# Gated mix of two attentions on one core: the rows of the q/k projection in another order, so that four of its five tiles are stored whole

## The chip, the core and the metric

The kernel runs on one core of one Trainium2 chip. The metric is device time in microseconds (us) for one execution. A core has five engines that each work through their own queue of instructions in order: TensorE (PE, matrix products; PEld is its loading of weights), VectorE (DVE), ScalarE (ACT), GpSimd (POOL), and SyncE (SP), which in this kernel issues every DMA. They wait for each other through semaphores.

## The reference

One input `x` (2048 tokens of 640 channels) goes through two attention blocks with 32 heads of 20 channels, and a sigmoid gate mixes the two results.

```python
def _A_ref(x, wq, wk, wv, wo, beta):          # 4 segments of 512 tokens
    q, k, v = x @ wq, x @ wk, x @ wv          # split into heads and segments
    phi = lambda t: where(t > 0, t + 1.0, exp(t))
    for s in range(4):
        p = softmax(qs @ ks.T * scale + mask) # inside the segment, key after query masked
        a_dot = p @ vs
        a_mem = (phi(qs) @ M) / (phi(qs) @ z + 1e-6)
        o = g * a_mem + (1 - g) * a_dot       # g = sigmoid(beta), one a head
        M, z = M + phi(ks).T @ vs, z + sum(phi(ks))
    return concat(o) @ wo
def _B_ref(x, wqkv, wo):                      # causal, window of 256 keys
    return softmax(windowed(q @ k.T * scale)) @ v @ wo
g = sigmoid((x * gate_w).sum(-1))
return g * a + (1 - g) * b                    # a, b: results of the two blocks
```

(Reshapes into heads and segments are left out.)

## The kernel before

**Tiles and units.** Work is cut by segment (`s`, 512 tokens) and by group of 16 heads (`g`: 0 and 1 are the two halves of block A, 2 and 3 of block B). One such pair is a T; there are 16, in the order g = 0, 2, 1, 3 in each segment. A T has four units `u` of four heads each, so 64 units. A T needs five q/k tiles `m` of 128 rows by 512 tokens (640 rows: 320 of q, 320 of k) and four v tiles.

**Exact products.** Most products run in a 32-bit format with fewer mantissa bits. Each operand is therefore split in a high part and a low rest (`split_h`, L516 or L518, and `split_l`, L532), and three products are added. `gemm2` (L578) and `v_mm` (L730) use only 64 of the array's 128 rows; two of them, one on each row half, run at the same time. Which instruction stands next to which in PE's queue thus decides whether both halves are filled. The probability times value product (`av_mm`, L919) and the small memory products (`mem_read` L946, `mem_add` L966) use strips of 128 x 32, and no half product runs beside them.

**From projection to scores.** A finished q/k tile goes from the accumulation bank to SBUF as a pair of parts, `ml[:, 0]` high (`m_high`, ACT, L599) and `ml[:, 1]` low (`m_low`, DVE, L603). SP stores it to DRAM in an image where every head has 20 rows high, 20 rows low and 20 rows high again; q holds high, low, high and k high, high, low, so that one product over 60 rows gives all three terms. The image has 160-row pieces, and tiles have 128 rows, so `runs_of` cuts a tile into one or two runs, eight in a T, and `qk_store` issues two DMAs for each run: L635 stores high and low to two places, L633 stores the high part again. That makes 16 DMAs for a T. `stack_read` (L804, L807, L809) reads a unit's rows back into `qks`. `max_mm` (L833) computes scores, `max_red` (L843, DVE) their row maxima, which go through DRAM (L859, L863) into two more rows of `qks`; `st_mm` (L887) then computes scores less the maximum, `st_exp` (L894, ACT) the exponential.

**Memory of block A.** `phi_neg`, `phi_exp`, `phi_sum` (L640, L644, L648) make phi of a q/k tile, `phi_store` (L657) writes it by the same runs to `dphi`, `mem_query` (L933) reads phi of q back in eight DMAs for two units, `mem_load` (L927) phi of k.

**Loading.** `load` (L524) brings weight tiles (`wst`, two buffers) and pieces of x (`xst`, four buffers); at the start the five pieces of the first segment go through the four `xst` buffers.

**What sets the order.** No loop order is written by hand. Each step is put into a list with a due time, an engine, a duration, and the buffers that it reads and writes; `Plan.order` then simulates the engines and takes, for the engine that can start first, the waiting step with the lowest rank. A rank is the due time, shifted by tables by kind of step and time (`SHIFT`, and `NUDGE` in slots of 12.5 us). The order in which steps are taken is the order of every queue. SP's queue has at most eight DMAs in flight: each waits for the one eight before it.

## Time and profile before

| | us |
|---|---|
| median of 3 runs | 988.43 |
| lowest, highest | 983.97, 991.27 |
| profiled execution, its own time | 980.1 |
| span of its instructions | 978.4 |
| PE, DVE, ACT, POOL busy | 967.9, 761.4, 651.7, 637.2 |
| PEld busy | 812.6 |
| granted clock | 1.000 |
| DMA | 248.56 MB, mean 254 GB/s |

The profile is of one execution. A row of a group gives the line, engine, operation, what is written and read, the count, then the busy time with the mean of one in ns, and then the engine's idle time just before, with what ended it. Ends of products on PE are modelled, and products on the two row halves overlap, so a PE that is busy all the time can still have one half empty.

### The profile page before, as it was taken

Reading aid. Unit: us, or ns where it says so; the run is one execution under the profiler, and the core shown is the slowest. Engines: PE = TensorE matmul, PEld = TensorE weight load, DVE = VectorE, ACT = ScalarE, POOL = GpSimd, SP = SyncE. Lnnn points to the kernel's source line nnn. Section 1 sums busy time; section 2 is a strip of 40 time slices with the busy share of each in tenths; the row PEclk is TensorE's granted clock in tenths of the full one; section 3 lists DMA queues with packets and bytes.
Section 4 is the critical chain, followed back from the end, with each engine's and each line's share of the span. In section 5 each row is a group of like instructions: output and inputs, shape, how many; then the busy total and the mean of one; then the engine's idle time right before and its main releaser. Section 6 shows DMA issues by size and latency. Waiting matters only on the chain.

```text
span 978.4 us, 30482 instructions
## 1 busy us (share of the span) xinstructions
PE 967.9 (99%) x11295; PEld 812.6 (83%) x11295; DVE 761.4 (78%) x2626; ACT 651.7 (67%) x1432; POOL 637.2 (65%) x864
## 2 busy tenths in 40 slices
...
GB/s 276 306 306 267 290 277 275 252 293 265 279 260 283 277 220 308 205 314 298 260 264 242 254 280 207 311 224 333 285 230 234 222 296 270 137 268 215 180 99 103
DMA packets 158036, 248.56 MB, mean 254 GB/s; under 512 B 52032, under 2 KB 68288, under 8 KB 157888
## 3 DMA queue, kind: packets, MB, share of 16 engines
...
## 4 chain that ended last, share of the span: by engine, by line
PE 92%; DVE 3%; DMA 3%; ACT 0%; issue 0%; POOL 0%; SPq 0%; DVEq 0%
PE bank L578 43%; PE bank L919 15%; PE bank L730 14%; PE bank L833 9%; PE bank L887 8%; DVE bank L843 2%; PE bank L570 2%; DMA wst<-wqk 1%; PE bank L946 1%; PE bank L966 1%; DMA wvs<-wv 1%; DMA xst<-xt 1%; DVE mx L843 0%; DVE ot L990 0%; SPq L524 0%
## 5 line engine op out<-in xcount | busy, mean ns | idle before, releaser
L894 ACT ACTIVATE P<-bank 128x512 f32<-128x512 f32 (+2 forms) x768 | 381.3, 556 | 148.2 <-PE bank L887 98.2
L578 PE MATMUL bank<-xhl,w 64*128 64x512 f32 x2400 | 453.5, 398 | 3.6 <-ACT xhl L516 2.8
L578 PEld LDWEIGHTS bank<-xhl,w 64*128 64x128 f32 x2400 | 325.4, 186 | 14.8 <-ACT xhl L516 3.7
L833 PE MATMUL bank<-qks 60*128 60x384 f32 (+3 forms) x1024 | 309.1, 334 | 1.3 <-DVE ot L990 0.8
L843 DVE CUSTOM_DVE_ANT_0 bank<-bank,mask_b 128x384 f32<-128x384 f32 (+2 forms) x512 | 259.7, 553 | 28.3 <-PE bank L833 21.1
L730 PE MATMUL bank<-wv,xhl 64*128 64x320 f32 (+1 forms) x1920 | 280.6, 313 | 0.2 <-POOL wv L532 0.2
L843 DVE CUSTOM_DVE_ANT_0 bank<-bank,mask_a 128x128 f32<-128x128 f32 (+3 forms) x512 | 239.9, 509 | 39.4 <-PE bank L833 29.2
L887 PE MATMUL bank<-qks 62*128 62x384 f32 (+3 forms) x1216 | 261.1, 301 | 0.4 <-DVE ot L990 0.2
L730 PEld LDWEIGHTS bank<-wv,xhl 64*128 64x128 f32 x1920 | 238.8, 186 | 3.2 <-issue 1.2
L578 PE MATMUL bank<-ohl,w 64*128 64x512 f32 x1050 | 226.3, 399 | 0.1
L532 POOL TENSOR_TENSOR w<-wst,w 128x640 fp32r<-128x640 f32 x112 | 174.9, 1565 | 77.9 <-ACT w L516 77.0
L900 POOL TENSOR_SCALAR_AFFINE_SELECT P<-P 128x512 f32<-128x512 f32 x256 | 161.5, 640 | 76.7 <-ACT P L894 71.6
L887 PEld LDWEIGHTS bank<-qks 62*128 62x128 f32 x1216 | 195.8, 185 | 15.3 <-issue 3.3
L833 PEld LDWEIGHTS bank<-qks 60*128 60x128 f32 x1024 | 177.5, 184 | 20.8 <-issue 6.2
L919 PE MATMUL bank<-P,vau 128*32 128x384 f32 (+3 forms) x2432 | 159.9, 407 | 0.2
L578 PEld LDWEIGHTS bank<-ohl,w 64*128 64x128 f32 x1050 | 152.9, 185 | 8.6 <-issue 3.3
L843 DVE DVE_READ_ACCUMULATOR2_ANT mx<- 128x1 f32 x1024 | 142.5, 139 | 0.0
L919 PEld LDWEIGHTS bank<-P,vau 128*32 128x32 f32 x2432 | 69.3, 110 | 78.6 <-issue 63.5
L516 ACT ACTIVATE w<-wst 128x640 fp32r<-128x640 f32 x121 | 89.4, 741 | 40.1 <-PE bank L578 15.7
L990 DVE STREAM_TRANSPOSE ot<-bank 128x512 f32<-128x512 f32 x64 | 45.8, 715 | 64.0 <-PE bank L919 61.6
L903 POOL TENSOR_SCALAR_AFFINE_SELECT P<-P 128x512 f32<-128x512 f32 x112 | 70.8, 641 | 4.5 <-ACT P L894 4.1
L532 POOL TENSOR_TENSOR wv<-wvs,wv 128x322 fp32r<-128x322 f32 x80 | 65.2, 834 | 11.8 <-ACT wv L516 11.5
...
## 6 DMA issues: line engine op xcount, KB each, us to landing
...
```

Of the source, the lines that this page charges most:

```text
L516: nc.scalar.activation(dst, src, AF.Copy)
L532: EN[e].tensor_tensor(out=t[:, 1], in0=B.pop(src), in1=f(t[:, 0]), op=ALU.subtract)
L578: z = nc.tensor.matmul(B[key], B[wkey][64 * r:64 * r + 64, a, 128 * c:128 * c + 128], B[xkey, c][64 * r:64 * r + 64, b], start=start, stop ...
L730: z = nc.tensor.matmul(B["v", T, b][:, :n], B[("x", s), c][64 * r:64 * r + 64, a, 128 * b:128 * b + 128], B["wv", T, c][64 * r:64 * r + 64 ...
L833: nc.tensor.matmul(psum(("mx", u, p, b, r))[:, :n], fr(q), keys(u, 3 * DH, r, p, c0, n), start=True, stop=True)
L843: nc.vector.tensor_tensor_reduce(out=x, in0=x, in1=mk, scale=1.0, scalar=BIG, op0=ALU.add, op1=ALU.max, accum_out=B["M", u][:, j:j + 1])
L887: nc.tensor.matmul(B[k][:, c:c + 128 * n], keys(u, K, r, p, WIN + 128 * kb, 128), fr(q[64 * r:64 * r + K, L * p + 128 * q0:L * p + 128 * ( ...
L894: nc.scalar.activation(B["P", u, b][:, 2 * r + p, c0:c1], B["st", u, b, p, r][:, c0:c1], AF.Exp, scale=SCALE)
L900: nc.gpsimd.affine_select(out=v, in_=v, pattern=[[0, 4], [1, 128]], compare_op=ALU.is_ge, fill=0.0, base=0, channel_multiplier=-1)
L903: nc.gpsimd.affine_select(out=v, in_=v, pattern=[[0, 4], [-1, 128]], compare_op=ALU.is_gt, fill=0.0, base=0, channel_multiplier=1)
L919: nc.tensor.matmul(o[32 * j:32 * j + 32, 128 * q0:128 * (q0 + n)], v[:, VA * h:VA * h + 32], t[:, j, c:c + 128 * n], start=(b == 0 and i = ...
L990: nc.vector.transpose(t, B["o", u])
```

## The change

The columns of the q/k weights are laid out anew, which gives the rows of the projection another order. For a group of 16 heads, tiles 0 and 1 now hold the first 16 channels of q, eight heads each (16 x 8 = 128 rows, one half of the image); tiles 3 and 4 the same for k. Tile 2 holds the last four channels of q (64 rows) and of k (64 rows).

- `qk_store`: a whole tile takes two DMAs. One writes the high part to its two places at once, by reading the same source twice; the other writes the low part. Tile 2 takes six DMAs of 64 rows. A T has 14 instead of 16, all T's together 224 instead of 256. The store of the high part no longer waits for `m_low`: a step may now ask for the `first` writer of a buffer alone.
- `phi_store`: one DMA a tile, two for tile 2 where both are wanted; 36 instead of 48. `mem_query`: six DMAs for two units instead of eight, 72 instead of 96. `dphi` and `mem_add` use the new row order.
- The five pieces of x for the first segment go into the five `ys` buffers, which are free then.
- The planner: `join` (a marker between the two halves of an accumulation) is planned shorter, `NUDGE` is looked up by finer groups of steps (`GROUPS`), and its numbers are all new. So the order of every queue is new.

The products, the conversions and the bytes of each are the same in number; SP's list falls from 1042 DMAs to 974.

```diff
--- before
+++ after
@@ -77,31 +77,44 @@
+GROUPS = dict(
...
-    a={22: 0.6},
...
+    c={7: 1.3, 31: -0.8, 32: -1.4, 39: 1.5, 66: 3.8},
...
@@ -238,6 +254,11 @@
                     deps[i] |= s["free"] if name[0] in ("qk", "qf", "pk") else {s["base"]}
                 s["puts"].append(i)
             for name in get:
+                if name[0] == "first":
+                    s = slot(name[1])
+                    deps[i].add(s["base"])
+                    s["gets"].append(i)
+                    continue
                 s = slot(name)
                 assert s["puts"] or s["base"] is not None, (fn, a, name)
                 deps[i] |= set(s["puts"])
...
@@ -520,6 +541,7 @@
 
     def load(tag, pool, bufs, width, key, src):
         B[key] = (xpool.tile([128, L], F32, name=tag, tag=tag, bufs=bufs)[:, :width] if tag == "xst" else
+                  work.tile([128, L], F32, name=tag, tag=tag, bufs=bufs) if tag == "ys" else
                   pool.tile([128, width], F32, name=tag, tag=tag, bufs=bufs))
         nc.sync.dma_start(B[key], src)
 
...
@@ -602,16 +624,9 @@
         t = B["ml", k]
         nc.vector.tensor_tensor(out=t[:, 1], in0=B[k], in1=f(t[:, 0]), op=ALU.subtract)
 
-    def runs_of(m, kinds=(0, 1)):
-
-        out, r = [], 0
-        while r < 128:
-            z, at = divmod(128 * m + r, QB)
-            n = min(QB - at, 128 - r)
-            if z // 2 in kinds:
-                out.append((*divmod(z, 2), at, r, n))
-            r += n
-        return out
+    PARTS = ((0, 0), (0, 1), None, (1, 0), (1, 1))
+    PIECES = [[(0, 128, 0), (0, 128, 1)], [(0, 128, 0), (0, 128, 1)], [(64 * w, 64, i) for i in range(3) for w in range(2)],
+              [(0, 128, 0), (0, 128, 1)], [(0, 128, 0), (0, 128, 1)]]
 
     def image(T, w):
 
...
@@ -622,17 +637,24 @@
         d = dkb[g - 2] if w else dqb[T // 2 % 2]
         return (d, S, d.offset + L * s) if w else (d, L, d.offset)
 
-    def qk_store(T, m, n, twice):
-
-        w, half, at, r, c = runs_of(m)[n]
+    def qk_store(T, m, n):
+
+        r, c, i = PIECES[m][n]
+        w, half = PARTS[m] or (r // 64, 0)
         d, row, off = image(T, w)
-        ml = f(B["ml", ("m", T, m)][r:r + c])
-        z = (2 - 2 * w) if twice else w
-        off += (512 * half + 8 * DH * z + at) * row
-        if twice:
-            nc.sync.dma_start(bass.AP(tensor=d.tensor, offset=off, ap=[[row, c], [1, L]]), ml[:, 0])
+        step = 8 * DH * row
+        if c == 128:
+            x = f(B["ml", ("m", T, m)])[:, i]
+            off += 512 * half * row + (2 - w) * step * i
+            if i:
+                nc.sync.dma_start(bass.AP(tensor=d.tensor, offset=off, ap=[[row, 128], [1, L]]), x)
+            else:
+                nc.sync.dma_start(bass.AP(tensor=d.tensor, offset=off, ap=[[row, 128], [(1 + w) * step, 2], [1, L]]),
+                                  bass.AP(tensor=x.tensor, offset=x.offset, ap=[list(x.ap[0]), [0, 2], [1, L]]))
         else:
-            nc.sync.dma_start(bass.AP(tensor=d.tensor, offset=off, ap=[[row, c], [8 * DH * row, 2], [1, L]]), ml)
+            x = f(B["ml", ("m", T, m)])[r:r + 64, i // 2]
+            off += 128 * row + ((0, 1 + w, 2 - w)[i]) * step
+            nc.sync.dma_start(bass.AP(tensor=d.tensor, offset=off, ap=[[row, 32], [512 * row, 2], [1, L]]), x)
 
 
     def phi_neg(T, m):
...
@@ -647,15 +669,17 @@
         e = B["phi", T, m]
         nc.vector.scalar_tensor_tensor(e, B["m", T, m], 0.0, e, op0=ALU.max, op1=ALU.add)
 
-    def phi_rows(T, m):
+    def phi_kinds(T):
         s = head(T)[1]
-        return runs_of(m, tuple(w for w in range(2) if (s < NSEG - 1 if w else s)))
-
-    def phi_store(T, m, n):
+        return [w for w in range(2) if (s < NSEG - 1 if w else s)]
+
+    def phi_store(T, m, w):
         d = dphi[head(T)[0]]
-        w, half, at, r, c = phi_rows(T, m)[n]
-        nc.sync.dma_start(bass.AP(tensor=d.tensor, offset=d.offset + (2 * QB * w + 2 * at + 4 * half) * L,
-                                  ap=[[8 * L, c // 4], [L, 4], [1, L]]), B["phi", T, m][r:r + c])
+        off = d.offset + 2 * QB * w * L
+        if PARTS[m]:
+            nc.sync.dma_start(bass.AP(tensor=d.tensor, offset=off + PARTS[m][1] * L, ap=[[2 * L, 128], [1, L]]), B["phi", T, m])
+        else:
+            nc.sync.dma_start(bass.AP(tensor=d.tensor, offset=off + 256 * L, ap=[[L, 64], [1, L]]), B["phi", T, m][64 * w:64 * w + 64])
 
     tiles = []
 
...
@@ -684,7 +708,7 @@
                         bank=("pj", NPP, k) if ph == n == 0 else (), mod=[k] if ph or n else [],
                         get=[wkey, (x, c)], pace=P0 if t < 4 else PACE, cols=256)
                 if ph == 0:
-                    add(t0 + NC * dt - 0.01, AD, (0.2, 0.08), join, k, mod=[k], off=-9)
+                    add(t0 + NC * dt - 0.01, AD, (0.06, 0.06), join, k, mod=[k], off=-9)
 
     def plan_qk(t, dt, e):
         T, m = e[0]
...
@@ -702,24 +726,19 @@
         ph, ml = ("phi", T, m), ("ml", ("m", T, m))
 
         add(t + 1e-4, ACT, 0.5, m_high, k, new=[("ml", 2, ml)], get=[k], off=EV)
-        add(t + 1.1e-4, DVE, 0.61, m_low, k, mod=[ml], get=[k], off=EV)
-        for n, z in enumerate(runs_of(m)):
-            for twice in range(2):
-                add(t + 3e-4, SP, 0.55, qk_store, T, m, n, twice, put=[("dq", T)] if m or n or twice else [],
-                    new=[] if m or n or twice else [(("dq", T % 4) if g < 2 else ("dq", T), 1, ("dq", T))],
-                    get=[ml], size=(4096, 2048)[twice] * z[4], packet=2048)
-        runs = phi_rows(T, m) if g < 2 else []
-        if runs:
-            zs = {w: min(x for x in range(NC) for y in phi_rows(T, x) if y[0] == w) for w in {z[0] for z in runs}}
-            new = [w for w in zs if zs[w] == m]
+        add(t + 1.1e-4, DVE, 0.61, m_low, k, put=[ml], get=[k], off=EV)
+        for n, (r, c, i) in enumerate(PIECES[m]):
+            add(t + 3e-4, SP, 0.55, qk_store, T, m, n, put=[("dq", T)] if m or n else [],
+                new=[] if m or n else [(("dq", T % 4) if g < 2 else ("dq", T), 1, ("dq", T))],
+                get=[("first", ml) if i == 0 or c == 64 and i == 1 else ml], size=(4096 if c == 128 and i == 0 else 2048) * c, packet=2048)
+        ws = [w for w in phi_kinds(T) if not PARTS[m] or PARTS[m][0] == w] if g < 2 else []
+        if ws:
             add(t + 4e-5, ACT, 0.5, phi_neg, T, m, new=[("phi", 2, ph)], get=[k], off=EV)
             add(t + 5e-5, ACT, 0.54, phi_exp, T, m, mod=[ph], off=EV)
             add(t + 6e-5, DVE, 0.61, phi_sum, T, m, get=[k], mod=[ph], off=EV)
-            for n, z in enumerate(runs):
-                w = z[0]
-                add(t + 7e-4, SP, 0.7, phi_store, T, m, n, get=[ph], size=2048 * z[4],
-                    new=[(("dphi", g, w), 1, ("dphi", T, w))] if w in new else [], put=[] if w in new else [("dphi", T, w)])
-                new = [x for x in new if x != w]
+            for w in ws:
+                add(t + 7e-4, SP, 0.6, phi_store, T, m, w, get=[ph], size=2 ** 18 if PARTS[m] else 2 ** 17,
+                    new=[(("dphi", g, w), 1, ("dphi", T, w))] if m == 2 * w else [], put=[] if m == 2 * w else [("dphi", T, w)])
 
     def v_mm(T, b, r, c, i, start, stop):
         if start:
...
@@ -930,9 +949,13 @@
     def mem_query(T, du, i, x):
 
         d, r = dphi[head(T)[0]], i // 2
-        nc.sync.dma_start(qfs[(2 * T + du) % NF][32 * i:32 * i + DH, x].rearrange("p (k t) -> p k t", k=2), bass.AP(
-            tensor=d.tensor, offset=d.offset + (8 * du + 2 * x + i % 2) * L + 256 * r,
-            ap=[[16 * L, DH], [4 * L + 256 * (1 - 2 * r), 2], [1, 256]]))
+        off = d.offset + (8 * du + 4 * x + 2 * (i % 2)) * L + 256 * r
+        if r:
+            nc.sync.dma_start(qfs[(2 * T + du) % NF][32 * i:32 * i + DH],
+                              bass.AP(tensor=d.tensor, offset=off, ap=[[16 * L, DH], [4 * L, 2], [1, L]]))
+        else:
+            nc.sync.dma_start(qfs[(2 * T + du) % NF][32 * i:32 * i + DH, x].rearrange("p (k t) -> p k t", k=2),
+                              bass.AP(tensor=d.tensor, offset=off, ap=[[16 * L, DH], [L + 256, 2], [1, 256]]))
 
     def mem_read(u):
 
...
@@ -1255,10 +1278,11 @@
         add(te, DVE, 0.64, o_turn, u, 0, get=[("o", u)], new=[("ot", 2, ok)])
         if not isb:
             if s > 0:
-                for j in range(8 * (1 - u % 2)):
+                for j, (i, x) in enumerate(((0, 0), (1, 0), (2, 0), (3, 0), (0, 1), (1, 1)) if u % 2 == 0 else ()):
                     qk = ("qf", u // 2)
-                    add(u + QF + 0.001 * j, SP, DI, mem_query, T, g // 2, j % 4, j // 4, get=[("dphi", T, 0)],
-                        new=[] if j else [("qf", NF, qk)], put=[qk] if j else [], size=DH * 2048, packet=1024, rings=10, late=DS)
+                    add(u + QF + 0.001 * j, SP, DI, mem_query, T, g // 2, i, x, get=[("dphi", T, 0)],
+                        new=[] if j else [("qf", NF, qk)], put=[qk] if j else [], size=(1 + i // 2) * DH * 2048, packet=1024 * (1 + i // 2),
+                        rings=10, late=DS)
                 add(te + 0.03, DVE, 0.72, o_turn, u, 1, get=[("num", u), ("nub", u)], put=[ok])
             if s < NSEG - 1:
                 for i in range(4 * (1 - u % 2)):
...
@@ -1294,7 +1318,10 @@
     for g in range(NSG):
         i, half = divmod(g, 2)
         cols = [w[:, 320 * half:320 * half + 320].reshape(D, 1, 4, 2, 2, DH) for w in (wq[i], wk[i])]
-        qk.append(np.concatenate(cols, 1).transpose(0, 1, 3, 5, 2, 4).reshape(D, QK))
+        cols = np.concatenate(cols, 1).transpose(0, 1, 3, 5, 2, 4)
+        most = cols[:, :, :, 0:16].reshape(D, 4, 128)
+        rest = cols[:, :, :, 16:].transpose(0, 1, 3, 4, 5, 2).reshape(D, 128)
+        qk.append(np.concatenate([most[:, 0], most[:, 1], rest, most[:, 2], most[:, 3]], 1))
         vv.append(np.concatenate([wv[i][:, 320 * half:320 * half + 320], n(gate_w)[:, None], zero], 1))
 
 
...
```

How this moves instructions is seen at three places. The first is the start of SP's queue: `wst` are weight tiles for the q/k projection, `xst` or `ys` pieces of x, `wvs` the v weights, `dqk`, `dqb`, `dkb` the images in DRAM (here their unused rows are filled from `ot`). Before:

```order
L524 DMA wst<-wqk 128x640
L524 DMA xst<-xt 128x512 x4
L442 DMA bet<-beta 128x1x8
L524 DMA wst<-wqk 128x640
L485 DMA dqk_108<-ot 128x128 x4
L524 DMA xst<-xt 128x512
L524 DMA wst<-wqk 128x640
L549 DMA wvs<-wv 128x5x322
L485 DMA dqb_110<-ot 128x128 x2
```

and now:

```order
L546 DMA wst<-wqk 128x640
L546 DMA ys<-xt 128x512 x5
L546 DMA wst<-wqk 128x640
L463 DMA bet<-beta 128x1x8
L506 DMA dqk_108<-ot 128x128 x2
L546 DMA wst<-wqk 128x640
L506 DMA dqk_108<-ot 128x128 x2
L571 DMA wvs<-wv 128x5x322
L506 DMA dqb_110<-ot 128x128 x2
```

The fifth piece of x stood behind four fillings and now follows the fourth at once; the third weight tile stands before two of the fillings.

The second is PE's queue after the warm-up products: `xhl` and `w` are the split x and q/k weights, `wv` the v weights. Before, and below it now:

```order
L578 MATMUL bank<-xhl,w 128x512 x52
L730 MATMUL bank<-wv_269,xhl 128x322
L578 MATMUL bank<-xhl,w 128x512 x3
L730 MATMUL bank<-wv_269,xhl 128x322
L578 MATMUL bank<-xhl,w 128x512
```

```order
L600 MATMUL bank<-xhl,w 128x512 x86
L749 MATMUL bank<-wv_285,xhl 128x322 x4
L600 MATMUL bank<-xhl,w 128x512 x2
L749 MATMUL bank<-wv_285,xhl 128x322 x2
L600 MATMUL bank<-xhl,w 128x512 x2
```

The first v product comes after 86 q/k products instead of 52, so the third weight tile is wanted before the v weights.

The third is SP's queue where the first T's q/k tiles are stored (`ml` is the pair of parts). Before:

```order
L635 DMA dqk_108<-ml 128x2x512
L549 DMA wvs<-wv 128x5x322
L524 DMA wst<-wqk 128x640 x2
L633 DMA dqk_108<-ml 128x512
L635 DMA dqk_108<-ml 32x2x512
L633 DMA dqk_108<-ml 32x512
L635 DMA dqk_108<-ml 96x2x512
L633 DMA dqk_108<-ml 96x512
L524 DMA xst<-xt 128x512 x4
```

and now:

```order
L652 DMA dqk_108<-ml 128x2x512
L506 DMA dqb_111<-ot 128x128 x2
L506 DMA dkb_113<-ot 128x512 x2
L546 DMA xst<-xt 128x512 x2
L546 DMA wst<-wqk 128x640
L650 DMA dqk_108<-ml 128x512
L652 DMA dqk_108<-ml 128x2x512
L650 DMA dqk_108<-ml 128x512
```

Two tiles take four stores instead of six; the first store of a tile (L652) is the high part for both places, and the low part (L650) follows.

66 lines of the change are left out of this document (40 added, 26 removed).

## The prediction

> **What bounds the kernel now.** I read the page first, then the groups of instructions, then busy time by stretches, then the start in order of time. The page:
>
> ```profile
> span 978.4 us, 30482 instructions
> PE 967.9 (99%) x11295; PEld 812.6 (83%) x11295; DVE 761.4 (78%) x2626; ACT 651.7 (67%) x1432; POOL 637.2 (65%) x864
> PE 92%; DVE 3%; DMA 3%; ACT 0%; issue 0%; POOL 0%; SPq 0%; DVEq 0%
> ```
>
> PE is busy for all but 10.5 us, and the chain that ended last (third row) is PE for 92%. SP's queue, which this change shortens, has 0% of it. So the change can win in two ways only: where PE is idle, and where PE counts as busy with one of its two row halves empty. How much of the second there is, I estimate from the groups:
>
> ```profile
> L578 PE MATMUL bank<-xhl,w 64*128 64x512 f32 x2400 | 453.5, 398 | 3.6 <-ACT xhl L516 2.8 <-DVE xhl L532 0.5 <-DVE mx L843 0.3
> L578 PE MATMUL bank<-ohl,w 64*128 64x512 f32 x1050 | 226.3, 399 | 0.1
> L730 PE MATMUL bank<-wv,xhl 64*128 64x320 f32 (+1 forms) x1920 | 280.6, 313 | 0.2 <-POOL wv L532 0.2
> L833 PE MATMUL bank<-qks 60*128 60x384 f32 (+3 forms) x1024 | 309.1, 334 | 1.3 <-DVE ot L990 0.8 <-DVE mx L843 0.2
> L887 PE MATMUL bank<-qks 62*128 62x384 f32 (+3 forms) x1216 | 261.1, 301 | 0.4 <-DVE ot L990 0.2
> L919 PE MATMUL bank<-P,vau 128*32 128x384 f32 (+3 forms) x2432 | 159.9, 407 | 0.2
> ```
>
> and from three runs of equal products in order of time:
>
> ```profile
> 26.56 3.85 PE L578 MATMUL bank<-xhl,w 64*128 64x512 f32 x31
> 39.31 1.94 PE L730 MATMUL bank<-wv,xhl 64*128 64x322 f32 x20
> 957.08 17.34 PE L570 MATMUL bank<-ohl,w 128*128 128x512 f32 x75
> ```
>
> With both halves fed, 31 products of 512 columns take 3.85 us; less the last one's 0.40, that is 3.45 / 30 = 0.115 us for one, and 0.225 ns a column. A v product takes (1.94 - 0.31) / 19 = 0.086. L833 and L887 have 340 and 286 columns in the mean (348,160 in all for each, by the widths in the code): 0.077 and 0.064 us. So 3450 x 0.115 = 397, 1920 x 0.086 = 165, 1024 x 0.077 = 79, 1216 x 0.064 = 78, L919 160, L570 17; the warm-up, L946 and L966 are about 30. Together 926. The span has 978.4. Of that the start loses some 4 to an idle PE (3.3 of the 3.6 us in the first group, and 0.8 before PE's first instruction), and after PE's last product, at 957.08 + 17.34 = 974.4, 4 more pass. About 44 us are left for everything that a better order could win in the middle: spread over 65 stretches between the L919 blocks, 0.7 us each. That is the ceiling, and it needs a perfect order.
>
> [...] PEld's 83% agrees that PE is not full; taken alone it would leave 17%, 166 us, an estimate far above the 44, because an L919 block loads little while it holds the array.
>
> **The start.** The rows that matter, in order of time:
>
> ```profile
> 7.35 1.99 ACT L516 ACTIVATE xhl<-xst 128x512 fp32r<-128x512 f32 x3 [2.25 <-DMA xst<-xt]
> 8.12 0.33 SPq L524 DMA_DIRECT2D xst<-xt  x1
> 8.76 2.14 PE L578 MATMUL bank<-xhl,w 64*128 64x512 f32 x16 [0.23 <-DVE xhl L532]
> 11.84 0.63 ACT L516 ACTIVATE xhl<-xst 128x512 fp32r<-128x512 f32 x1 [1.64 <-DMA xst<-xt]
> 12.52 0.50 PE L578 MATMUL bank<-xhl,w 64*128 64x512 f32 x2 [1.62 <-ACT xhl L516]
> 13.25 3.65 PE L578 MATMUL bank<-xhl,w 64*128 64x512 f32 x27 [0.23 <-DVE xhl L532]
> ```
>
> The fifth piece of x is issued at 8.12, behind four fillings, lands for 11.84, and PE waits 1.62 + 0.23 = 1.85 us for its two parts. The change issues it right behind the fourth. ACT then converts it straight after the three others, at 7.35 + 1.99 = 9.3 to 10.0, and DVE by 10.7; PE wants it at 10.5. So 1.85 us go, at most 0.2 remain. The next candidate is the third weight tile, wanted after 60 products, that is 30 x 0.115 = 3.5 us after 11.2, at 14.7; it is now issued before two fillings, so I take it as landed in time. **Term: -1.9**, between 0 (see the rivals) and -2.3.
>
> **The stores.** A store pair takes SP some 1.2 us:
>
> ```profile
> 196.04 0.50 SPq L635 DMA_DIRECT2D dqk<-ml  x1
> 196.59 0.70 SPq L633 DMA_DIRECT2D dqk<-ml  x1
> ```
>
> 68 DMAs fewer (32 q/k, 12 phi, 24 phi queries) at 0.5 to 0.7 are 34 to 48 us of SP's queue. SP is not on the chain, so this counts for nothing by itself. It counts where a load that PE wants stands behind stores. The chain shows the dearest such place:
>
> ```profile
> 214.64 5.94 DMA wst<-wqk
> 220.61 0.75 ACT w L516
> 221.43 1.55 POOL w L532
> ```
>
> ```profile
> 224.06 0.32 PE L833 MATMUL bank<-qks 60*128 60x128 f32 x1 [0.83 <-DVE ot L990]
> ```
>
> A weight tile arrives late, POOL's small subtraction of a maximum waits behind its split, and PE ends up idle for 0.83. All idle time that PE has between the start and the end is 10.5 - 4 - 4 = 2 to 3 us. I take a third of it, **-0.8**, between -2.5 and +2.5. The high part stored before the low one is ready saves up to one L603:
>
> ```profile
> L603 DVE TENSOR_TENSOR ml<-bank,ml 128x512 fp32r<-128x512 f32 x80 | 53.5, 680 | 24.9 <-ACT ml L599 18.6 <-ACT phi L640 5.4 <-PE bank L887 0.8
> ```
>
> 0.68 us for the earliest store; but `stack_read` waits for all 14 stores, the low ones too, so I count **0**. What hides it is that PE has q/k or v products of another T to do meanwhile; without them it would be 0.68 for each of 16 T's, 11 us either way. The phi transfers and `mem_query` are off the chain as well: 0. Conversions, products and bytes are the same: 0.
>
> [...]
>
> **The new order.** This decides. I counted in both programs which row half each product uses. Between two L919 blocks the two halves get unequal columns: the differences sum to 47,376 columns before and 41,464 now. The shorter half waits; against an even split, half the difference is lost: 5,912 x 0.225 ns = 1.3 us less lost. Also 1061 products stood behind another one for the same half, now 933. Each such place can empty the other half for up to one product: 128 x 0.115 = 15 us if all of them did, 0 if the next product was always early enough. Nearest to the truth are the 44 us that are lost at all: 44 x 128 / 1061 = 5. Between 1.3 and 5, **-3**. But order also decides whether data are ready, and this no count shows: bounds +10 and -10.
>
> **Sum.** -1.9 - 0.8 - 3 = -5.7. The profiled execution took 980.1 (its span and 1.7 around it); it would take 974.4. The median of the runs is 8.3 above the profiled one, and I take that as the same for both: 988.4 - 5.7 = 982.7, so **983**.
>
> **Rivals.** *The order gains more (A).* If readiness improves too, because fewer stores stand before loads, a quarter of the 44 goes with the start: -11 - 1.9 = -13, **975**. For it: PE has 44 us to give, and the two counts go the right way. Against it: a quarter is much when the halves' columns improve by an eighth.
>
> *The start gives nothing (B).* In the stretch behind it the DMAs are as full as PE:
>
> ```profile
> 16.50:75.00 58.50, 58.33 (x615) 56.52 (x615) 26.66 (x91) 25.07 (x57) 26.15 (x26) 1.00 0.96 311
> 75.00:100.00 25.00, 24.19 (x262) 18.11 (x251) 22.42 (x85) 18.77 (x44) 13.86 (x18) 1.00 0.86 254
> 200.00:300.00 100.00, 99.13 (x1208) 82.88 (x1207) 88.71 (x339) 74.85 (x176) 63.47 (x93) 1.00 0.89 277
> 900.00:925.00 25.00, 24.85 (x236) 17.89 (x234) 24.66 (x87) 14.58 (x33) 20.13 (x28) 1.00 0.58 180
> ```
>
> (columns: stretch, length, busy PE, PEld, DVE, ACT, POOL, clock, DMA share, GB/s). At 0.96 and 311 GB/s, PE that is 1.9 us early would wait for weights, and only -3.8 stays: **985**. PE's 58.33 of 58.50 says that DMA is not late yet.
>
> *PE waits for DVE (C), the other side.* DVE has 22.4 of 25 us at 75 and 24.7 of 25 at 900. A unit costs DVE 10 us of maxima:
>
> ```profile
> L843 DVE CUSTOM_DVE_ANT_0 bank<-bank,mask_b 128x384 f32<-128x384 f32 (+2 forms) x512 | 259.7, 553 | 28.3 <-PE bank L833 21.1 <-PE bank L578 3.0 <-PE bank L887 1.0
> L843 DVE CUSTOM_DVE_ANT_0 bank<-bank,mask_a 128x128 f32<-128x128 f32 (+3 forms) x512 | 239.9, 509 | 39.4 <-PE bank L833 29.2 <-PE bank L578 3.4 <-PE bank L730 3.1
> L843 DVE DVE_READ_ACCUMULATOR2_ANT mx<- 128x1 f32 x1024 | 142.5, 139 | 0.0
> ```
>
> (642 / 64), and there is one bank for each row half. Where the order puts several L833 behind each other without other products, PE goes at DVE's pace:
>
> ```profile
> 75.13 1.58 PE L833 MATMUL bank<-qks 60*128 60x256 f32 x6
> 76.99 0.92 PE L578 MATMUL bank<-xhl,w 64*128 64x512 f32 x2 [0.28 <-DVE mx L843]
> ```
>
> Six took 76.99 - 75.13 = 1.86 us where both halves fed would take 6 x 0.077 = 0.46: 1.4 lost. One such place in each of the 16 T's is +22, less the 5.7: **+17, 1005**. It decides from (10 + 5.7) / 1.4 = 11 places on. For it: the stretches to 300 leave DVE a tenth of its time. Against it: counted in both programs, the first L833 of each T stands within 8 us of PE work of its old place, so DVE's density hardly changes.
>
> That the change doesn't do what it says is not a rival: SP's rows show the two-store tiles and the five pieces.
>
> **Chances.** Forecast 0.43 (979 to 988 of its own), A 0.28, B 0.13, C 0.16 (from 998 at its eleventh place to 1005 at sixteen). About 1%, 9.9 us, can be told from no change, as three runs of one kernel lie 983.97 to 991.27. Faster by over 1% (under 978.5) is A with a part of it short of that and the forecast's lower edge: 0.29. Slower by over 1% is C: 0.16. Within: 0.55. The range reaches to the beginning of C and past A to a third of the 44 us (988.4 - 15 - 1.9 = 971): 971 to 998, with 2 in 10 left out.
>
> **What would show it.** In the profile of the changed kernel: PE's first products without a wait over 0.5 us after the fourth piece of x (right) or a wait for `wst` at about 14 (B); SP with 974 DMAs and SPq still at 0% of the chain; PE busy minus the same product counts, with the chain's DVE share at or below 3% (C would raise it, and show runs of L833 with `mx` as the releaser); the stretch from 200 to 300 with PEld above its 82.88 of 100 (A: above 86). Wrong would be a gain that sits in SP or DMA, or a start that is as late as before.

## The result and the profile after

The changed kernel takes 976.52 us (median of 6 runs, 975.36 to 980.36), the kernel before beside it 987.22 (6 runs, 983.77 to 991.27): a ratio of 0.990 with a 95% interval of 0.987 to 0.993. On a second chip the ratio was 0.993 (0.991 to 0.995). So the change is worth 7 to 10 us. (Differences between two kernels are taken below from their ratios to before, times 985 us; differences of the medians stand beside them where they tell another size.)

The two profiles show nothing of this. The page of the kernel after, its span, its busy times and the shares of its chain of waits:

```profile
span 978.6 us, 30474 instructions
PE 967.6 (99%) x11295; PEld 810.2 (83%) x11295; DVE 757.3 (77%) x2623; ACT 644.5 (66%) x1436; POOL 637.7 (65%) x863
PE 89%; DMA 4%; DVE 3%; ACT 1%; issue 1%; SPq 1%; POOL 1%; DVEq 0%; ACTq 0%; POOLq 0%
```

The span is 978.6 against 978.4, PE's busy time 967.6 against 967.9. The profiled execution of after took 980.36 us, the slowest of its six; that of before took 980.1, and of the 107 runs of before that were timed beside the kernels of this study, on five chips, one was shorter (980.06). One profile met an unlucky execution, the other a lucky one. A second profile of the changed kernel (978.1 us) is used beside the first below.

The groups of instructions of after, by line, with busy time, mean ns and the idle time ahead of them:

```profile
L600 PE MATMUL bank<-xhl,w 64*128 64x512 f32 x2400 | 446.3, 398 | 1.4 <-POOL w L554 0.6 <-ACT ml L621 0.3 <-DVE xhl L554 0.2
L749 PE MATMUL bank<-wv,xhl 64*128 64x320 f32 (+1 forms) x1920 | 272.0, 313 | 0.0
L852 PE MATMUL bank<-qks 60*128 60x384 f32 (+3 forms) x1024 | 304.3, 332 | 2.5 <-DMA qks<-dkb 0.7 <-DVE mx L862 0.7 <-DVE den L1022 0.5
L906 PE MATMUL bank<-qks 62*128 62x384 f32 (+3 forms) x1216 | 260.0, 304 | 1.4 <-DVE mx L862 1.2
```

The 3.6 us ahead of the q/k products, most of it at the start, have become 1.4. The products of the maxima (L852) and of the scores (L906) now wait 2.5 and 1.4 where it was 1.3 and 0.4, partly for DVE's maxima. The start, in order of time:

```profile
1.24 2.31 SPq L546 DMA_DIRECT2D ys<-xt  x5
7.54 3.13 PE L600 MATMUL bank<-xhl,w 64*128 64x512 f32 x22 [0.23 <-DVE xhl L554]
7.84 1.24 ACT L537 ACTIVATE xhl<-ys 128x512 fp32r<-128x512 f32 x2 [0.35 <-DMA ys<-xt]
10.87 6.63 PE L600 MATMUL bank<-xhl,w 64*128 64x512 f32 x56 [0.19 <-ACTq L615]
```

No wait over 0.5 us is left, and the 56 products run through. The same stretches as before (length, busy PE, PEld, DVE, ACT, POOL, clock, DMA share, GB/s):

```profile
0.00:16.50 16.50, 15.14 (x106) 10.71 (x108) 6.39 (x13) 8.24 (x15) 4.86 (x18) 1.00 0.88 283
16.50:75.00 58.50, 57.69 (x596) 53.02 (x592) 27.83 (x100) 23.34 (x54) 25.51 (x26) 1.00 0.95 314
75.00:100.00 25.00, 24.57 (x287) 18.85 (x275) 22.49 (x84) 19.81 (x46) 12.91 (x17) 0.93 0.86 248
200.00:300.00 100.00, 99.92 (x1251) 83.07 (x1251) 88.93 (x333) 72.96 (x177) 64.50 (x91) 1.00 0.87 273
900.00:925.00 25.00, 24.86 (x250) 18.80 (x247) 24.68 (x87) 15.75 (x35) 20.37 (x28) 1.00 0.57 177
```

and the first of before, which has 78 products where after has 106:

```profile
0.00:16.50 16.50, 12.40 (x78) 8.00 (x80) 6.76 (x11) 7.54 (x13) 5.68 (x19) 1.00 0.82 255
```

The start gives 28 more products in 16.5 us, but in the second stretch less gets done: PEld was 56.52 of 58.50 and is 53.02, PE 58.33 and is 57.69. In the third the clock is 0.93. Why shows in a finer cut of after:

```profile
75.00:79.50 4.50, 4.17 (x33) 2.41 (x20) 4.30 (x20) 3.85 (x8) 2.14 (x2) 0.99 0.91 281
79.50:82.90 3.40, 3.40 (x20) 2.79 (x20) 3.31 (x12) 3.34 (x10) 1.16 (x2) 0.50 0.74 158
82.90:90.00 7.10, 7.00 (x105) 5.55 (x104) 5.45 (x23) 3.25 (x7) 3.92 (x5) 1.00 0.90 257
```

From 75 to 79.5 us PE gets through few products (33 in 4.5 us, PEld 2.41), since DVE, busy for 4.30 of it, holds the banks of the maxima (this is read from DVE's busy time; the idle time of PE that ends with DVE's maxima is only 0.16 us there). Then 3.40 us run at a clock of 0.50, which costs up to 1.7.

This is not the new order's alone. From 75 to 100 us the clock is 0.93 in both profiles of the change and in those of `after_late_x`, `after_fill_late`, `old_order_new_stores` and `old_order_new_all` below, and 0.86 in that of `new_order_old_stores`; in `after_low_big` it is 0.83 from 80 to 90 us. In both profiles of before it is 1.00 from 75 to 100 us. The old order with the new stores, `old_order_new_stores` below, shows the half clock behind the six products of the maxima that before runs at 75.13, where the clock stays at 1.00:

```profile
76.00:79.90 3.90, 3.46 (x47) 1.91 (x45) 3.90 (x18) 1.47 (x3) 3.10 (x3) 1.00 0.83 320
79.90:83.30 3.40, 3.40 (x21) 3.31 (x21) 2.48 (x13) 0.00 (x0) 0.16 (x1) 0.51 0.32 97
```

For orientation, what all runs measured, as ratios to before on the same chip, and in us of 985:

```
                        ratio   95% interval     against before
change                  0.9897  0.9865..0.9929   -10.1
change, second time     0.9926  0.9907..0.9945    -7.3
before, second time     0.9999  0.9979..1.0018    -0.1
start_only              0.9992  0.9974..1.0011    -0.8
old_order_new_stores    0.9968  0.9953..0.9984    -3.2
old_order_new_all       0.9961  0.9939..0.9983    -3.8
new_order_old_stores    1.0058  1.0033..1.0084    +5.7
after_late_x            0.9968  0.9951..0.9985    -3.2
after_high_twice        0.9944  0.9923..0.9965    -5.5
after_phi_split         0.9954  0.9935..0.9973    -4.5
after_rows_split        0.9948  0.9929..0.9967    -5.1
after_low_big           0.9937  0.9913..0.9960    -6.2
after_fill_late         0.9905  0.9874..0.9937    -9.4
```

### The profile page after: what moved, and what is told of

The parts are those of the page before. It is cut to its first block, busy times and chain, and to the rows that moved or that the text cites. A ratio compares the mean times of both kernels' runs of the same rounds, so it can differ in the third digit from the quotient of the medians.

```text
span 978.6 us, 30474 instructions
## 1 busy us (share of the span) xinstructions
PE 967.6 (99%) x11295; PEld 810.2 (83%) x11295; DVE 757.3 (77%) x2623; ACT 644.5 (66%) x1436; POOL 637.7 (65%) x863
## 2 busy tenths in 40 slices
DMA packets 156276, 248.56 MB, mean 254 GB/s; under 512 B 51232, under 2 KB 65568, under 8 KB 156128
## 3 DMA queue, kind: packets, MB, share of 16 engines
q1 hardware_dynamic: 156128, 246.62, 79.2%
## 4 chain that ended last, share of the span: by engine, by line
PE 89%; DMA 4%; DVE 3%; ACT 1%; issue 1%; SPq 1%; POOL 1%; DVEq 0%; ACTq 0%; POOLq 0%
PE bank L600 40%; PE bank L938 15%; PE bank L749 14%; PE bank L852 8%; PE bank L906 8%; DVE bank L862 2%; PE bank L592 1%; PE bank L969 1%; DMA wst<-wqk 1%; DMA qks<-dkb 1%; PE bank L989 1%; DMA wvs<-wv 1%; DMA ys<-xt 1%; DVE ys L1093 0%; DMA qfs<-dphi 0%
## 5 line engine op out<-in xcount | busy, mean ns | idle before, releaser
L913 ACT ACTIVATE P<-bank 128x512 f32<-128x512 f32 (+2 forms) x768 | 376.7, 559 | 136.4 <-PE bank L906 101.6
L600 PE MATMUL bank<-xhl,w 64*128 64x512 f32 x2400 | 446.3, 398 | 1.4 <-POOL w L554 0.6
L600 PEld LDWEIGHTS bank<-xhl,w 64*128 64x128 f32 x2400 | 320.3, 186 | 13.8 <-DVE xhl L554 1.6
L852 PE MATMUL bank<-qks 60*128 60x384 f32 (+3 forms) x1024 | 304.3, 332 | 2.5 <-DMA qks<-dkb 0.7
L749 PE MATMUL bank<-wv,xhl 64*128 64x320 f32 (+1 forms) x1920 | 272.0, 313 | 0.0
L862 DVE CUSTOM_DVE_ANT_0 bank<-bank,mask_a 128x256 f32<-128x256 f32 (+3 forms) x512 | 239.5, 512 | 34.8 <-PE bank L852 21.2
L906 PE MATMUL bank<-qks 62*128 62x384 f32 (+3 forms) x1216 | 260.0, 304 | 1.4 <-DVE mx L862 1.2
L749 PEld LDWEIGHTS bank<-wv,xhl 64*128 64x128 f32 x1920 | 230.9, 186 | 2.6 <-ACT P L913 0.5
L600 PE MATMUL bank<-ohl,w 64*128 64x512 f32 x1050 | 224.0, 398 | 0.0
L906 PEld LDWEIGHTS bank<-qks 62*128 62x128 f32 x1216 | 194.4, 186 | 21.0 <-issue 5.8
L852 PEld LDWEIGHTS bank<-qks 60*128 60x128 f32 x1024 | 177.8, 185 | 20.4 <-issue 4.5
```

The costliest lines, as they stand in the source:

```text
L600: z = nc.tensor.matmul(B[key], B[wkey][64 * r:64 * r + 64, a, 128 * c:128 * c + 128], B[xkey, c][64 * r:64 * r + 64, b], start=start, stop ...
L749: z = nc.tensor.matmul(B["v", T, b][:, :n], B[("x", s), c][64 * r:64 * r + 64, a, 128 * b:128 * b + 128], B["wv", T, c][64 * r:64 * r + 64 ...
L852: nc.tensor.matmul(psum(("mx", u, p, b, r))[:, :n], fr(q), keys(u, 3 * DH, r, p, c0, n), start=True, stop=True)
L862: nc.vector.tensor_tensor_reduce(out=x, in0=x, in1=mk, scale=1.0, scalar=BIG, op0=ALU.add, op1=ALU.max, accum_out=B["M", u][:, j:j + 1])
L906: nc.tensor.matmul(B[k][:, c:c + 128 * n], keys(u, K, r, p, WIN + 128 * kb, 128), fr(q[64 * r:64 * r + K, L * p + 128 * q0:L * p + 128 * ( ...
L913: nc.scalar.activation(B["P", u, b][:, 2 * r + p, c0:c1], B["st", u, b, p, r][:, c0:c1], AF.Exp, scale=SCALE)
```

## The experiments

### The kernel before once more, and the parts alone

Four kernels shared a chip. The first is before, unaltered.

> The kernel before, unchanged, profiled once more. Its first profile was of an execution of 980.1 us, below all six timed runs (983.8 to 991.3). Theory A (that execution was an unusually good one, and what the change removes is something that most executions of the kernel before meet and that one did not): this profile shows 983 to 991 us, and against the first one it shows more idle PE, or a stretch at half clock, that adds up to 4 to 10 us. Theory B (profiling changes the time, and the first profile is typical for a profiled execution): about 980 us again, with the same rows. Ratio to the kernel before: 1.00 within 0.4%.

Measured: 983.89 us (981.07 to 987.16), ratio 0.9999. So 0.2% can be told apart here. Its profiled execution took 983.9 us, 3.8 more than the first one, which is theory A; the late transfer below accounts for 3.5 us of it. Its profile shows how two executions of one program differ. From the chain of waits:

```profile
827.24 8.40 DMA xst<-o_dram
836.19 0.59 ACT P L894
```

The busy times of the stretches around it, in the columns of above:

```profile
830.00:833.70 3.70, 3.70 (x48) 3.63 (x47) 1.52 (x9) 3.38 (x7) 3.49 (x4) 1.00 0.76 244
833.70:837.10 3.40, 1.55 (x20) 1.29 (x19) 1.14 (x4) 1.45 (x4) 2.63 (x4) 1.00 0.43 133
837.10:840.50 3.40, 3.40 (x25) 3.40 (x25) 2.78 (x8) 2.49 (x6) 3.14 (x4) 0.50 0.21 79
840.50:844.00 3.50, 3.50 (x39) 3.42 (x37) 2.38 (x11) 3.16 (x8) 1.55 (x4) 1.00 0.14 26
```

An output piece landed late (8.40 us in the chain), ACT stood in front of its split, the exponential behind it came late (at 836.19), PE was idle for 1.85 us, and the next 3.4 us ran at half clock (0.50): an estimated 3.5 us from one late transfer, 1.85 and half of 3.4. The first profile of before has no such place.

The start alone, in the order of before:

```diff
+        steps = [(fn, a) for fn, a, _ in self.order()]
+        first = [i for i, (fn, a) in enumerate(steps) if fn.__name__ == "load" and a[4][0][0] == ("x", 0)]
+        late = steps.pop(first[4])
+        steps.insert(first[3] + 1, late)
...
```

> The order of the kernel before in every queue, with its stores; alone the fifth piece of the first x is loaded right behind the fourth, into a ys buffer. Theory 'start': PE's wait of 1.62 + 0.23 us at 12.5 us goes and the rest follows 1.9 us earlier: 985.3 where before is 987.2 (ratio 0.998). Rival 'the DMA-filled stretch behind it takes it back': PE's waits at the start go, and PE idles or has empty halves more by as much before 75 us: ratio 1.000.

Measured: 982.44 us, ratio 0.9992: nothing. The load was earlier, but ACT and DVE kept their order, in which the fifth piece's split stands behind the next weight's and the gate's steps, and PE still waited 0.82 + 1.15 us:

```profile
11.64 0.51 PE L583 MATMUL bank<-xhl,w 64*128 64x512 f32 x2 [0.82 <-ACT xhl L520]
13.30 3.42 PE L583 MATMUL bank<-xhl,w 64*128 64x512 f32 x26 [1.15 <-DVE xhl L537]
```

So this run doesn't test the start of the change, only the earlier load.

The stores and phi transfers alone, in the order of before (each old step issues the new DMA that answers to it, or none):

```diff
-    plan.emit()
+    seen = {}
+    for fn, a, _ in plan.order():
+        if fn is qk_store:
+            T, m, n, twice = a
+            j = seen[T, m] = seen.get((T, m), -1) + 1
+            for k in (((0, 1), (2, 3), (4,), (5,)) if m == 2 else ((0,), (1,), (), ()))[j]:
+                new_qk_store(T, m, k)
...
```

> The new row order, whole-tile stores, fewer phi transfers and fewer phi queries, but every queue keeps the order of the kernel before: where it had a store, there is one or none. The start is that of before. Theory 'order' (the gain is the planner's new order): no change within 2 us, ratio 0.998 to 1.002. Theory 'transfers' (68 fewer DMAs on SP let loads go out earlier, and PE meets fewer late operands): 4 to 10 us less, ratio 0.990 to 0.996, with fewer waits of PE for unit data and weights.

Measured: 980.81 us, ratio 0.9968 (0.9953 to 0.9984), -3.2 us with an interval of -1.6 to -4.6. That is a gain, below the 4 to 10 of the theory 'transfers'.

The order and the start alone, with the old layout and DMAs (each new step issues the old ones that answer to it):

```diff
-    plan.emit()
+    for fn, a, _ in plan.order():
+        if fn is qk_store:
+            T, m, n = a
...
+                for k in range(len(runs_of(m))):
+                    old_qk_store(T, m, k, 1 - n)
...
```

> The order of the changed kernel in every queue and its start, but the old row order of the q/k weights, the old runs of rows, 256 stores, 48 phi stores and 96 phi queries: each old DMA stands where the new one for the same rows stood. Theory 'order': the gain stays, ratio 0.988 to 0.993. Theory 'transfers': the gain goes, ratio 0.997 to 1.003; and since this order was made for fewer DMAs, PE may wait for late loads in it and be slower than before by some us.

Measured: 990.46 us (980.99 to 995.19), ratio 1.0058 (1.0033 to 1.0084): slower than before by 5.7 us, and slower than the whole change by 13 to 16. The order alone loses, the DMAs alone gain 3.2, together they gain 7 to 10: the terms don't add up. Where part of it goes, the waits of the engines in its profile say (waiting engine and line, what released it, us in total, times, longest):

```profile
ACT w L537 <- DMA wst<-wqk: 15.0, 13, 2.8
...
ACT ohl L537 <- DMA xst<-o_dram: 10.0, 8, 2.8
...
PE bank L940 <- ACT P L947: 3.5, 5, 1.6
...
PE bank L886 <- ACT P L947: 1.2, 1, 1.2
```

and the same rows of the changed kernel's second profile:

```profile
ACT ohl L537 <- DMA xst<-o_dram: 6.3, 4, 2.5
...
ACT w L537 <- DMA wst<-wqk: 4.4, 5, 1.6
...
PE bank L852 <- ACT P L913: 1.1, 1, 1.1
```

ACT waits 25 us for weights and output pieces instead of 11. (In the first profile of the change these two rows are 6.7 + 8.0 = 14.7. In the old order they are 12.0 and 12.3 in the two profiles of before, and with the new stores 7.4 and, in `old_order_new_all` below, 11.3.) These loads stand on SP behind the stores and go through the same DMA queue (q1, which moved 246.62 of the 248.56 MB in the first profile of before); the exponentials stand behind the loads' splits on ACT; PE waits for the exponentials. PE's idle time ahead of maxima and scores is 8.7 us (3.0 and 5.7) where the second profile of the change has 2.9 (2.6 and 0.3), and the half clock near 80 us lasts 6.8 us instead of 3.4. These two come to some 7.5 us, over half of the 13; the rest is not found.

### Parts undone in the changed kernel

Four kernels shared a second chip. The first is the changed kernel, unaltered.

> The changed kernel once more, with nothing altered, beside the three others of this group. Its first profile took 980.36 us, the slowest of its six executions (median 976.52), and showed a stretch of half clock at 79.5 us that cost about 1.7 us. If the gain of 10 us is real, the median is again 975 to 978, ratio about 0.990. If the first comparison was a chance of the chip, it lies at 980 to 984. Theory 'late transfers': a profile at the median has fewer or shorter gaps of PE behind 400 us than the first profile of it (+1 to +3.5 us there against before).

Measured: 976.07 us (974.92 to 979.55), ratio 0.9926. The gain is real. Its profile took 978.1 us, so it is no profile at the median; that gaps are fewer there than in the first one is taken up in the last part.

The fifth piece of x issued late again:

```diff
...
+        pads = [i for i, (fn, a) in enumerate(steps) if fn.__name__ == "init_pad"]
+        late = steps.pop(first[4])
+        steps.insert(pads[3], late)
```

> The changed kernel in its own order, but the fifth piece of x is issued on SP behind the first four fillings, where it stood before the change; all other instructions in all queues stay. Theory 'start counts' (first step of the prediction, -1.9): PE again waits 1.6 to 2 us before 14 us, and the median is 2 to 3.5 us above that of the changed kernel, 978.5 to 980. Theory 'start given back' (rival B): the median is the same within 1 us, since what PE waits at the start it does not wait at 60 to 80 us.

Measured: 981.25 us, ratio 0.9968, 4.1 us above the changed kernel (5.2 by the medians). The start counts, and for more than its wait:

```profile
8.25 0.33 SPq L551 DMA_DIRECT2D ys<-xt  x1
8.88 1.52 PE L605 MATMUL bank<-xhl,w 64*128 64x512 f32 x10 [0.22 <-DVE xhl L559]
12.13 0.63 ACT L542 ACTIVATE xhl<-ys 128x512 fp32r<-128x512 f32 x1 [3.24 <-DMA ys<-xt]
12.82 0.50 PE L605 MATMUL bank<-xhl,w 64*128 64x512 f32 x2 [2.42 <-ACT xhl L542]
14.95 9.06 PE L605 MATMUL bank<-xhl,w 64*128 64x512 f32 x56 [0.19 <-ACTq L620]
```

PE is idle for 2.42 + 0.23, and then the 56 products that took 6.63 us in the changed kernel take 9.06. The clock of the stretch behind the wait is 0.71, and in a closer cut 0.50 for 6.8 us:

```profile
14.50:24.00 9.50, 9.31 (x61) 8.16 (x61) 2.35 (x5) 4.52 (x10) 3.01 (x4) 0.71 0.68 221
13.30:20.10 6.80, 6.38 (x30) 4.93 (x30) 2.23 (x6) 1.76 (x5) 1.58 (x2) 0.50 0.91 293
```

So here the late piece costs 2.6 us of waiting and at least 2.4 of half clock. In the first profile of before the same piece cost 1.62 + 0.23 us of waiting and nothing in clock, which is 1.00 up to 16.5 us there.

Four runs put the number of DMAs, their rows and their bytes back one by one. The high store as two stores (64 DMAs more):

```diff
-                nc.sync.dma_start(bass.AP(tensor=d.tensor, offset=off, ap=[[row, 128], [(1 + w) * step, 2], [1, L]]),
-                                  bass.AP(tensor=x.tensor, offset=x.offset, ap=[list(x.ap[0]), [0, 2], [1, L]]))
+                for k in range(2):
+                    nc.sync.dma_start(bass.AP(tensor=d.tensor, offset=off + k * (1 + w) * step, ap=[[row, 128], [1, L]]), x)
```

> The changed kernel in its own order, but the store of the high part of a whole tile, which puts it to both places at once, is two stores behind each other: 64 DMAs more on SP's queue, the same bytes, layout and packets. Theory 'queue length': the new order with the old 68 DMAs lost 14 us against the changed kernel (990.46 against 976.52), 0.2 us for each, so 64 more lose 8 to 13: 985 to 990. Theory 'shape of the stores' (what counts is that a tile is stored whole, not the number): 0 to 3 us, 976 to 980.

Measured: 978.17 us, ratio 0.9944, 1.8 us above the changed kernel, where differences under about 2.7 can't be told from noise. Each of the 64 DMAs costs about 0.03 us, and not the 0.2 of the theory 'queue length': their number by itself is not the 13 us. The phi transfers cut in two (48 DMAs more):

```diff
-            nc.sync.dma_start(bass.AP(tensor=d.tensor, offset=off + PARTS[m][1] * L, ap=[[2 * L, 128], [1, L]]), B["phi", T, m])
+            for k in range(2):
+                nc.sync.dma_start(bass.AP(tensor=d.tensor, offset=off + (PARTS[m][1] + 128 * k) * L, ap=[[2 * L, 64], [1, L]]),
+                                  B["phi", T, m][64 * k:64 * k + 64])
...
```

> The changed kernel in its own order, but each phi store of 128 rows is two of 64, and each query load of two halves is two loads: 48 DMAs more on SP's queue, the same bytes and packets. Theory 'queue length': 48 x 0.2 = 10 us, if each DMA on SP's queue costs the same wherever it stands: 983 to 988. Theory 'the stores before a stack only': the phi transfers stand where nothing urgent waits behind them: 0 to 3 us, 976 to 980 (the prediction counted them at 0).

Measured: 980.02 us, ratio 0.9954, 2.8 us above the changed kernel (4.0 by the medians). That is at the edge of what can be told, and nearer to 'the stores before a stack only' than to the 10 us of 'queue length'. On another chip, tiles 1 and 3 stored in 32 and 96 rows (64 DMAs more):

```diff
+            for r0, r1 in {1: ((0, 32), (32, 128)), 3: ((0, 96), (96, 128))}.get(m, ((0, 128),)):
+                y = x[r0:r1]
...
```

> The changed kernel in its own order and layout, but the two stores of tiles 1 and 3 are cut by rows into 32 and 96, as before the change: 64 DMAs more, as many as when the high stores were doubled (+1.8 us), and the same bytes and packets. Theory 'number of DMAs': 0.9944 of before again, 1 to 3 us above the changed kernel (0.990 to 0.993). Theory 'pieces of unequal rows load the 16 DMA engines unequally' (what is left open of the 13 us that the old stores cost in the new order): 5 to 8 us above, 0.997 to 1.000.

Measured: 980.11 us, ratio 0.9948, 2.2 us above the second measurement of the change. The cut by rows costs about what the doubled high stores cost, within some 2.7 us; the 5 to 8 us of unequal pieces didn't come. And the same number of stores, but with 512 of 768 KB behind the low part:

```diff
             if i:
-                nc.sync.dma_start(bass.AP(tensor=d.tensor, offset=off, ap=[[row, 128], [1, L]]), x)
+                nc.sync.dma_start(bass.AP(tensor=d.tensor, offset=off + (1 - w) * step, ap=[[row, 128], [step, 2], [1, L]]),
+                                  f(B["ml", ("m", T, m)]))
...
```

> The changed kernel in its own order and layout and with the same number of stores, but of a whole tile the first store puts the high part to one place only, and the second puts the high part to its other place together with the low part. So 512 KB of the 768 KB of a tile leave behind DVE's subtraction, not 256. Theory 'the bytes that wait for the low part' (my term of 0 is wrong: the stack is read later): between the 1.8 us that 64 DMAs more cost and the 13 us that the old stores cost in this order, about +6: 980 to 984. Theory 'number only': the same within 1 us, 975 to 977.

Measured: 980.5 us, ratio 0.9937, 1.1 us above the change by the ratio of the second chip, and 3.2 (3.8 by the medians) above the kernel with the late fillings, which ran on its own chip (0.9905, below). The +6 isn't seen, though the two intervals leave room for 4. So each of the four undone by itself measured 1 to 3 us by the ratios, and only the phi transfers reach the edge of the noise; together with the old layout all old DMAs cost 13. The sum of the four is 8, though two of them add 64 stores each where the old kernel has 32 more.

### All but the order, and the full DMAs

These shared a third chip. Everything of the change but the new order:

```diff
...
+    for kind, at in ((load, 4), (split_h, 5), (split_l, 1)):
+        z = [i for i, (fn, a) in enumerate(steps) if fn is kind and (a[at][0] if kind is load else a[at])[0] == ("x", 0)]
+        late = steps.pop(z[4])
+        steps.insert(z[3] + 1, late)
```

> The order of before in every queue, but with the new layout, its stores and its phi transfers, and with the whole new start: the fifth piece of x is issued behind the fourth, and ACT and DVE split it right behind the fourth too. It is all of the change except the new order. The stores in the old order alone measured 0.9968; the start, measured in the new order by undoing it, 0.9968 against 0.9926, or 4 us. Theory 'parts add up, the new order is worth nothing by itself': 0.9968 - 0.0042 = 0.9926, about 977 us, the same as the changed kernel. Theory 'the new order is worth something' (the prediction's -3, and the 2.5 us that the two profiles of the changed kernel gain between 873 and 921 us): 0.995 to 0.997, 980 to 981.

Measured: 982.22 us, ratio 0.9961 (0.9939 to 0.9983), the same as without the new start. The theory that the parts add up falls. In its start the wait only moved on:

```profile
8.24 3.19 PE L579 MATMUL bank<-xhl,w 64*128 64x512 f32 x22 [0.22 <-DVE xhl L533]
8.58 0.33 SPq L525 DMA_DIRECT2D wst<-wqk  x1
12.90 0.74 ACT L516 ACTIVATE w<-wst 128x640 fp32r<-128x640 f32 x1 [1.55 <-DMA wst<-wqk]
13.69 4.18 PE L579 MATMUL bank<-xhl,w 64*128 64x512 f32 x22 [2.26 <-ACT w L516]
```

The fifth piece is there, and PE stands for 2.26 us before the third weight tile instead, issued at 8.58 behind four fillings. The new order issues it at 6.17, behind two:

```profile
6.17 0.34 SPq L546 DMA_DIRECT2D wst<-wqk  x1
```

So the start's gain needs the new order, and the new order is worth 3 to 6 us on top of the rest (0.9961 against 0.9926 and 0.9897). The two overlap: the early place of the third weight tile belongs to the new order, so these 3 to 6 us hold the start's.

Last, half of the fillings taken out of the early stretch, to see whether full DMAs are why the change loses time at 60 to 80 us:

```diff
+        pads = [z for z in pads if z[1][0] not in [y[1][0] for y in pads[:8]]]
+        steps = [z for z in steps if z not in pads]
+        for k, z in enumerate(pads):
+            at = next(i for i, (fn, a) in enumerate(steps) if fn.__name__ == "max_rows" and a == (1 + k // 2, 1))
+            steps.insert(at + 1 + k % 2, z)
...
```

> The changed kernel, but the eight fillings of the second set of images (0.9 MB), which nobody reads before 129 us, are issued between 80 and 116 us from a small tile of their own and not at 11 to 20 us. In both profiles of the changed kernel PE runs full from 30 to 60 us and loses 2 us against before at 60 to 80: ACT waits 2.95 us for the pieces of wv at 57.6, issued at 41.7 into DMAs that are 0.96 to 1.00 busy, and POOL and PE follow. Theory 'the full DMAs give the start back' (rival B): 0.9 MB at 325 GB/s are 2.8 us less of backlog, ACT's wait goes, and the median falls by 2 to 4 us, to 972 to 974, below both kernels. Theory 'DVE's maxima set the pace there' (rival C): DVE is busy all the time from 69 to 82 us whatever the DMAs do, and the median is the same within 1 us.

Measured: 976.69 us, ratio 0.9905, the same as the change. ACT's wait is still there, at 57.24 with the fillings late, from the timeline of that kernel:

```profile
57.24 0.92 ACT L551 ACTIVATE wv<-wvs 128x322 fp32r<-128x322 f32 x2 [2.94 <-DMA dkb<-ml]
```

and at 57.65 in the change, from its own:

```profile
57.65 0.93 ACT L537 ACTIVATE wv<-wvs 128x322 fp32r<-128x322 f32 x2 [2.95 <-DMA dkb<-ml]
```

With 0.9 MB less in front of it the wait has the same length. So these 0.9 MB are not what sets it. The DMAs are 0.99 busy from 40 to 50 us in both profiles, and 0.96 (change) and 0.94 (fillings late) from 50 to 60, so whether later transfers set it isn't shown. ACT's step reads `wvs`, not the `ml` store that the profile names as its releaser. No version that was run beats the change.

### Where the order gains and loses

To compare profiles whose executions differ by chance, I summed PE's products in order of their start, each by its columns at the rate of two fed halves, and read off when each sum was reached. Against the mean of the two profiles of before, the time that passed between two sums changed by (us; the sums 20 to 60 are passed at 28 to 70 us, 350 to 450 at 391 to 498, 800 to 840 at 873 to 922):

```
sum of work from..to    0..10   20..60  350..450  650..750  800..840
before, two profiles    ±0.6     0.0      0.0       ±0.2      0.0
old_order_new_stores    +2.1     0.0     -0.2        0.0     +0.1
old_order_new_all       +1.5     0.0     -0.2        0.0     +0.3
change, first profile   -2.9    +2.1     +1.1       -0.4     -2.5
change, second profile  -2.1    +2.0     +1.1       -1.0     -2.6
after_late_x            +3.6    +2.1     +1.1       -0.9     -2.5
after_high_twice        -2.4    +2.0     +1.2       -0.5     -2.5
after_phi_split          0.0    +2.1     +1.4       -0.8     -2.5
after_fill_late         -2.6    +2.0     +1.0       -0.8     -2.5
new_order_old_stores    -2.5    +2.8     +1.4       +0.1     -2.5
```

The new order loses 2.0 between 50 and 70 us in every kernel that has it and 1.1 near 470, gains, with the new stores, 0.4 to 1.0 between the sums 650 and 750, and gains 2.5 between 873 and 922, where the stretch from 900 to 925 above has PEld at 18.80 and had it at 17.89 before. These four places cancel. With the start, 2.1 to 2.9 earlier than before, this makes about -3, nearly all of it the start. The table leaves out most of the sums from 60 to 800; there two executions of one program differ by as much as the whole gain: by 5.0 us for before's two profiles and by 3.8 for the change's (the second is ahead). So profiles of single executions can't show the rest of the 7 to 10 us, and it shows in no single place. It may be in how often something lands late: the shortest runs of before and after differ by 5.1 us (980.06 of 107 and 974.92 of 12), the medians by 8.7, and the middle half of before's runs is some 4 us wide where nine of twelve of after lie within 2. That rarer late transfers are this rest is argued from the spread and from the one late piece that a profile caught, not shown. Half clock carries little of it: beside each other on one chip the mean granted clock was 0.9963 for before and 0.9977 for the change, and by the 0.9 us for each 0.001 that before's runs on this chip show, that is an estimated 1.3 us.

## Why the prediction was right, and which of its steps were not

The forecast was 983 with 971 to 998. The runs gave 976.5: on the gaining side, between the forecast's own 979 to 988 and rival A's 975, where the prediction had put a chance of 0.29 (under 978.5). The gain, called 5.7 us, is 7 to 10. The signs, of less waiting at the start and of fewer DMAs on SP, came; SPq, to stay at 0% of the chain, has 1% in the first profile after and 0% in the second.

**The start: the mechanism was right, the size was not.** The wait went, as foreseen, with no wait over 0.5 us left, and the third weight tile was the next candidate, as foreseen. Against the two profiles of before, the changed kernel passes the first sum of work 2.1 to 2.9 us sooner, a little over the -1.9; undoing the start in the new order cost 4.1. What the sum left out is the clock behind a wait: behind 2.4 us of idle PE it was 0.50 for 6.8 us, and the 56 products took 9.06 us instead of 6.63, though behind the 1.62 of before's first profile it was 1.00. How many runs of before pay this isn't known. The sum also counted the start as a term by itself. Without the two fillings that the new order moved behind the weight tile it was worth nothing: 0.9961 with the new start against 0.9968 without.

**The stores, phi and the high part first: -0.8 with two zeros was too little.** All of these in the old order measured -3.2 (-1.6 to -4.6), more than -0.8 and perhaps more than the -2.5 that I had set as the bound. The prediction's last sign, that a gain that sits in SP or DMA would be wrong, speaks against this step too. The step that failed is "SP is not on the chain, so this counts for nothing by itself", taken further to zeros for phi and for the high part. A chain of one lucky execution with SPq at 0% doesn't show the loads that stand behind stores in other executions; ACT's waits for q/k weight tiles and output pieces do in the new order: 25 us with the old stores, 11 to 15 with the new. In the old order they fall less clearly, from 12 to 7 or 11, so what the 3.2 us there are made of isn't shown. Singly, the parts are 1 to 3 us each, near what can be told apart.

**The new order: -3 came near by luck, and is not a term that can stand alone.** On top of everything else it is worth 3 to 6 us, but this holds the start, which the sum had counted already. Its reason, that the two row halves are filled more evenly, isn't shown: the four places away from the start where the order repeatedly gains or loses cancel. With the old DMAs it loses 5.7, and the ±10 that I had put on readiness covers this, but the sum treated the order and the DMAs as independent, and they are not.

**C, PE waits for DVE, didn't decide.** At 75 to 79.5 us the maxima hold PE up, and 3.40 us at half clock follow. But before has its run of maxima there too, which the prediction shows, and the half clock stands behind it in the old order with the new stores as well, so this is not the new order's doing; that the clock stays full there in before (1.00 from 79.5 to 82.9 us) isn't explained. C needed eleven places; the DVE share of the chain stayed at 3%, as said. **B** fell: the start's gain stays, as undoing it costs 4.1. The 2 us that the new order loses between 50 and 70 us are lost with the late piece of x too, so they don't come from the start, and not from the 0.9 MB of fillings, since they are lost without them there. Whether full DMAs count is open, as these stayed full. Whether ACT's order or DVE's pace sets them stays open too. PEld from 200 to 300 us was to exceed 82.88 and is 83.07, far from A's 86, so A's reason (a gain spread over the middle) is not what happened either, though its number was the nearest.

**The median stands 8.3 above the profile "for both": wrong.** The profiled execution of before was nearly its best of 107, that of after its worst. It also hid the gain when the two traces were laid side by side.

What stays open: four parts undone one by one cost 8 us in sum, all DMAs of before in the new order cost 13 to 16. The remaining 5 or more may be the parts' interplay or the old layout, which wasn't tried by itself, or in part noise, as each of the four carries some 2.7 us of it.
